# A recurrent segment kernel on one core: another order of the items of a segment, and three edits in front of the segment loop

## The chip, the cores and the metric

The kernel runs on one core of a Trainium2 chip. The metric is the device time of one launch in microseconds (us). A core has TensorE (PE, matrix products; its weight loads are listed as PEld), VectorE (DVE), ScalarE (ACT), GpSimd (POOL) and SyncE (SP, which here only issues DMA transfers). Each engine works off its own list of instructions in order, and they wait for each other by semaphores. PSUM, where TensorE leaves its products, has eight banks; ScalarE and VectorE copy ("evacuate") them to the on-chip memory SBUF.

## What is computed

```python
def _A_ref(x, mem0, Wq, Wk, Wv, Wo, seg_len):      # x (1, 2048, 640), 32 heads of 192, 8 memory rows, seg_len 32
    L = M + seg_len
    mask = (idx[:, None] < M) | (idx[:, None] >= idx[None, :])
    mem = mem0
    for s in range(n_seg):                          # 64 segments, one after the other
        h = jnp.concatenate([mem, xs], axis=1)      # 40 rows
        q, k, v = h @ Wq, h @ Wk, h @ Wv            # 640 -> 32 x 192 each
        p = _softmax(where(mask, q k^T * scale, -1e9))
        o = einsum(p v, Wo)                         # 6144 -> 640
        mem = o[:, :M, :]                           # the memory of the next segment
        outs.append(o[:, M:, :])

g = _sigmoid((x * gate_w).sum(-1, keepdims=True))
a = _A_ref(x, A_mem0, A_Wq, A_Wk, A_Wv, A_Wo, 32)
b = (_gelu(x @ w_gate) * (x @ w_up)) @ w_down       # the FFN, 640 -> 1536 -> 640
return g * a + (1 - g) * b
```

Part "a" is a recurrence: a segment needs the 8 memory rows which the segment before left. Part "b" depends on nothing but the input.

## The kernel before

**In front of the loop.** The FFN is done first, in four blocks (`blk`) of 512 rows, and left in device memory. `ffn_transposes` (line 818, DVE) makes five transposed input tiles `xT[k]`; `ffn_gu` makes for each of twelve column tiles f a gate product G (line 828), an up product U (line 831), a GELU (line 834, ACT) and their product `hT[f]` (line 836, DVE); `ffn_down` (line 850) multiplies all twelve `hT` by `w_down` for four row tiles `a`, each one PE operation with 24 matmuls. A PE operation waits, ahead of its first matmul, for everything it reads: the first G for all five `xT`, "down 0" for all twelve `hT`.

**Main rows and left rows.** A segment has 40 rows: 24 rows of x and 8 of memory (32 "main" rows), and the last 8 rows of x, which are called "left" rows. The left rows of four segments make a group g of 32 rows. Since they don't depend on the memory, their Q and K products are made ahead, as fill, one "unit" (group, octet) at a time, and kept in a scratch in device memory; a loop over `units` in front of the segments makes the first six of them (`left_mm`, line 919; `left_rows`, evacuation on ACT, transposes on DVE). The left V products are made once for four segments, in the segment with q = s % 4 = 0 (`proj`, second loop), but those of its first octet already in the segment before, as items "vb" (`vl_mm`, line 1092). Segment 0 has none before it and makes its own in its group 1, evacuated by DVE (`vl_evac`, line 1086).

**The segment loop.** 64 segments; heads go in four octets of eight, from 0 to 3 in even segments and from 3 to 0 in odd ones. A segment runs through a list of items, written out by hand or by a search: `PROG` for q = 0, 1, 2 and `PROG3` for q = 3. The code walks the list and hands each item's operations to the engines' queues, so the list is the order on every engine at once, and of the DMA issues on SP too:

- `g n k`: step k of five of the projection group n. `GROUPS` says which: group 0 is Q and K of octet 0, group 1 V of octet 0 with Q and K of octet 1, group 2 V 1 with Q 2 and K 2, group 3 V 2 and Q 3, group 4 K 3, group 5 V 3. Each of a group's products is four matmuls of 32-wide tiles side by side (line 1119, and line 226 where the weights stay). After step 4 ACT evacuates Q and K (line 1140) and V (line 1143).
- `tq i`, `tk i`: DVE transposes the Q or K rows of octet i (line 1154), POOL copies a part of Q (line 1157).
- `sc i`: scores of octet i on PE (lines 1165 to 1180), maximum and subtraction on DVE (lines 1192, 1194); POOL fills in the left Q and K of the next octet (line 976). `ex i`: exponential on ACT (line 1204), sum and normalization on DVE (line 1206 and on).
- `pt i`: transposes of the probabilities on PE (lines 1227 and 1232), evacuated by ACT (line 1245; octet 3 partly by DVE). `pv i`: probabilities times V with 64-wide tiles (lines 1260, 1262), evacuated to "U" by ACT (line 1278; octet 3 partly by DVE, line 1283).
- `wo i 0`, `wo i 1`: half of the output product of octet i; 64-wide in q = 3 (line 1339, where main and left rows go together), 32-wide else (line 1296; line 1321 for octet 3).
- `lf q u k`, `le q u m`: step k of a left unit, and its evacuation, in segments with that q only. `vb k`: as above, in q = 3.

**The seam.** After the last item, DVE and ACT collect the output product (lines 1506, 1509), DVE transposes the new memory rows into the input of the next segment (line 1517) and PE goes on with its first projections.

**The weights.** Not all of Wq, Wk, Wv and Wo fits into SBUF: 13 pieces of Q, K, V (384 KB each) and 3 of Wo (480 KB each) of octet 0 share their places with those of octet 3. As soon as a piece has been used for the last time in a segment, `swap_loads` issues on SP the load of the piece that shares its place (`load_piece`, line 628), so that every segment loads 16 pieces. An octet that ends a segment begins the next, so its pieces are there.

**PSUM banks** are dealt out in list order: `misc_bank` takes the bank which was given out longest ago among those free for that use.

Of the kernel before, what the change touches and what calls it, by code (L numbers as in the profile page):

```python
# [3 lines left out]
ACTF = mybir.ActivationFunctionType  # L4
# [234 lines left out]
def _build(nc, A_x, A_mem0, A_Wq, A_Wk, A_Wv, A_Wo, seg_len, w_gate, w_up, w_down,  # L239
           gate_w, out, opts=None):  # L240
    opts = dict(opts or {})
    Bsz, S, Dm = A_x.shape
# [274 lines left out]
    def piece_view(key, o):  # L517
        if key[0] == 3:
# [4 lines left out]
    PROG = [("g", 0, 0), ("g", 0, 1), ("g", 0, 2), ("g", 0, 3), ("g", 0, 4), ("tq", 0), ("g", 1, 0), ("g", 1, 1),  # L523
# [12 lines left out]
    PROG3 = [("g", 0, 0), ("g", 0, 1), ("g", 0, 2), ("g", 0, 3), ("g", 0, 4), ("g", 1, 0), ("tq", 0), ("tk", 0),  # L536
# [285 lines left out]
    def ffn_gu(blk):  # L822
        for f in range(FT):
            if blk + 1 == NFB and f and f % (FT // NH) == 0:
# [3 lines left out]
            S_.add("pe", [lambda e, k=k, f=f, gb=gb: e.matmul(ps[:, gb, 0:FB], wg_sb[NH * f // FT][:, k, f * 128 % FH:f * 128 % FH + 128], xT_sb[:, k, :],  # L828
                                                              start=(k == 0), stop=(k == KT - 1)) for k in range(KT)],
                   reads=[r_wg[NH * f // FT]] + r_xT, writes=[r_ps[gb]], name="ffn G %d %d" % (blk, f))  # L830
# [12 lines left out]
    def ffn_down(blk):  # L843
        n1 = min(Dm, 512)
        for a in range(FA):
            xb = 3 + 2 * (a % 2)
            yb = xb + 1
            fns = []
            for f in range(FT):
                fns.append(lambda e, f=f, a=a, xb=xb: e.matmul(ps[:, xb, 0:n1], hT_sb[:, f, a * 128:(a + 1) * 128], wd_sb[:, f, 0:n1],  # L850
                                                               start=(f == 0), stop=(f == FT - 1)))
                if Dm > 512:
                    fns.append(lambda e, f=f, a=a, yb=yb: e.matmul(ps[:, yb, 0:Dm - 512], hT_sb[:, f, a * 128:(a + 1) * 128], wd_sb[:, f, 512:Dm],
                                                                   start=(f == 0), stop=(f == FT - 1)))
            wr = [r_ps[xb]] + ([r_ps[yb]] if Dm > 512 else [])
# [89 lines left out]

    units = [(0, NOCT - 1)] + [(1, o) for o in LUNIT[3].values()] + [(0, 1), (0, 2), (0, 0)]
    for n, (g, o) in enumerate(units):
# [10 lines left out]
        left_store(g, o, b)  # L958
        if n == 0:
# [120 lines left out]
    def vl_evac(s, o, bk, eng="dve"):  # L1080
        out, in_ = vl_sb[o].rearrange("p (c n) -> p c n", c=3), ps[:, bk, 0:384].rearrange("p (n c) -> p c n", c=3)
        if eng == "act":
            S_.add("act", lambda e: e.activation(out=out, in_=in_, func=ACTF.Copy),
                   reads=[r_ps[bk]], writes=[r_vl[o]], name="Vl evac s%d o%d" % (s, o))
        else:
            S_.add("dve", lambda e: e.tensor_copy(out=out, in_=in_),  # L1086
                   reads=[r_ps[bk]], writes=[r_vl[o]], name="Vl evac s%d o%d" % (s, o))

    def vl_mm(s, k):
# [519 lines left out]
```

## Time and profile before

| | us |
|---|---|
| runs before: 1717.53, 1730.37, 1730.9; median | 1730.37 |
| the profiled execution, its time | 1724.01 |
| its span | 1722.3 |
| granted TensorE clock, mean | 0.995 |
| in front of the first segment | 177.3 |
| segments 0 to 62 | 1507.5 |
| segment 63, the last | 37.5 |

The lower three rows are windows of the profiled execution, cut at the first matmul of segments 0 and 63. Line numbers in the profile are those of the kernel before. A row of the profile's windows gives, for a stretch of time, the busy time of each engine and its number of instructions, then the granted clock (1 is full speed), the share of time in which the 16 DMA engines were busy, and what they moved. A row of the timeline gives start, duration, engine, line, operation, output and input, their shapes, how many instructions were put together, and in brackets the idle time in front and what ended it. A row of the waits gives engine, line, what it waited for, total us, how often, and the longest.

### The profile page before, as it was taken

The numbers are of one execution on the slowest core, as the hardware profiler recorded it, in microseconds if no ns is written. First come the engines' busy times: TensorE is split into PE (matmuls) and PEld (weight loads), VectorE is DVE, ScalarE is ACT, GpSimd is POOL, SyncE is SP. The second block draws the span as 40 slices with busy tenths as digits, with TensorE's granted clock in tenths as the row PEclk, the third lists the DMA queues.
The fourth block names the chain that finished last, engine by engine and source line by source line (L and its number), as shares of the span: only waits on it lengthen the run. The fifth ranks groups of instructions, "written<-read, shape, count | busy, mean of one in ns | idle before, by whom it ended". The sixth has DMA issues, their size and how long they took to land.

```text
span 1722.3 us, 75547 instructions
## 1 busy us (share of the span) xinstructions
PE 1587.5 (92%) x37107; PEld 778.1 (45%) x28147; DVE 1003.5 (58%) x2976; ACT 776.6 (45%) x1825; POOL 548.6 (32%) x1609
## 2 busy tenths in 40 slices
PE   9999899999999999999999899999999999999986
PEld 4444345444444444454444444454544444444443
DVE  5552666566565665655656656566665656555653
ACT  2222454545454454445444444445444544445442
POOL 1100233233333233333333333333333332333332
PEclk9999999999999999999999999999999999999998
DMA  9915988988888898879888898888888888988884
GB/s 298 326 37 153 342 311 296 322 308 297 297 299 319 307 323 281 305 276 329 295 287 302 294 333 281 283 288 319 310 298 288 296 316 289 310 280 303 314 313 170
DMA packets 278102, 499.27 MB, mean 290 GB/s; under 512 B 113951, under 2 KB 139015, under 8 KB 277767
## 3 DMA queue, kind: packets, MB, share of 16 engines
q1 hardware_dynamic: 249928, 482.45, 81.0%
q10 hardware_dynamic: 27839, 11.99, 2.5%
q8 instruction: 255, 4.18, 1.0%
q14 instruction: 80, 0.66, 0.1%
HBM read 473.25 MB, written 21.09 MB: 287 GB/s over the span
## 4 chain that ended last, share of the span: by engine, by line
PE 73%; DMA 12%; DVE 6%; ACT 4%; issue 3%; POOL 1%; SPq 0%; POOLq 0%; DVEq 0%; ACTq 0%
PE ps L1119 20%; PE ps L226 18%; DMA arena<-in_A_Wo_dram 6%; PE ps L1339 6%; PE ps L1296 5%; PE ps L1260 3%; PE ps L831 3%; PE ps L828 3%; PE ps L1165 3%; DMA arena<-in_A_Wv_dram 3%; PE ps L850 2%; PE ps L919 2%; PE ps L1173 1%; DMA arena<-in_A_Wk_dram 1%; ACT arena L1143 1%
## 5 line engine op out<-in xcount | busy, mean ns | idle before, releaser
L1119 PE MATMUL ps<-arena 128*32 128x384 bf16 x8660 | 650.9, 329 | 57.7 <-DVE arena L1517 47.4
L226 PE MATMUL ps<-arena 128*32 128x384 bf16 x8960 | 651.4, 326 | 7.7 <-DVE arena L1086 1.1
L1119 PEld LDWEIGHTS ps<-arena 128*32 128x32 bf16 x8660 | 221.7, 96 | 422.2 <-issue 265.6
L1154 DVE STREAM_TRANSPOSE arena<-arena 128x384 bf16<-128x384 bf16 x512 | 274.6, 561 | 125.8 <-ACT arena L1140 124.8
L1140 ACT ACTIVATE arena<-ps 128x384 bf16<-128x384 f32 x512 | 230.3, 493 | 233.8 <-PE ps L1119 223.3
L1296 PE MATMUL ps<-arena 128*32 128x320 bf16 x3456 | 187.1, 299 | 14.7 <-issue 13.4
L1157 POOL COPY arena<-arena 64x160 bf16<-64x160 bf16 x256 | 81.3, 318 | 374.3 <-DVE arena L1154 366.7
L1278 ACT ACTIVATE arena<-ps 128x480 bf16<-128x480 f32 (+1 forms) x256 | 137.6, 537 | 119.3 <-PE ps L1262 116.4
L1192 DVE TENSOR_REDUCE arena<-ps 104x4 f32<-104x160 f32 x256 | 82.9, 324 | 162.7 <-PE ps L1180 162.7
L1143 ACT ACTIVATE arena<-ps 128x384 bf16<-128x384 f32 x256 | 124.8, 488 | 106.9 <-PE ps L1119 105.3
L1245 ACT ACTIVATE arena<-ps 128x448 bf16<-128x448 f32 x192 | 104.6, 545 | 125.8 <-PE ps L1232 125.8
L1204 ACT ACTIVATE ps<-ps 104x160 f32<-104x160 f32 x256 | 75.8, 296 | 139.0 <-DVE ps L1194 137.1
L1206 DVE TENSOR_REDUCE arena<-ps 104x4 f32<-104x160 f32 x256 | 82.4, 322 | 95.7 <-ACT ps L1204 94.6
L976 POOL COPY arena<-arena 128x96 bf16<-128x96 bf16 x256 | 71.4, 279 | 201.2 <-PE ps L1180 163.8
L1296 PEld LDWEIGHTS ps<-arena 128*32 128x32 bf16 x3456 | 97.4, 96 | 68.2 <-issue 26.2
L1339 PE MATMUL ps<-arena 128*64 128x320 bf16 x1536 | 124.6, 305 | 1.2 <-ACT arena L1278 0.9
L1286 POOL COPY arena<-arena 128x96 bf16<-128x96 bf16 x192 | 51.3, 267 | 228.8 <-ACT arena L1278 222.6
L1260 PE MATMUL ps<-arena 128*64 128x160 bf16 x1536 | 118.3, 240 | 3.4 <-issue 3.3
L919 PE MATMUL ps<-arena 128*32 128x384 bf16 x1280 | 110.4, 328 | 0.0
L1262 PE MATMUL ps<-arena 128*64 128x64 bf16 x1536 | 104.2, 193 | 1.6 <-issue 1.3
L1260 PEld LDWEIGHTS ps<-arena 128*64 128x64 bf16 x1536 | 81.5, 109 | 47.5 <-ACT arena L1143 19.7
L1339 PEld LDWEIGHTS ps<-arena 128*64 128x64 bf16 x1536 | 79.9, 111 | 34.2 <-issue 10.4
(100 smaller groups left out, 2320.6 us busy)
## 6 DMA issues: line engine op xcount, KB each, us to landing
arena<-in_A_Wk_dram SPq DMA_DIRECT2D x335, 384.0 KB, 6.6
arena<-in_A_Wv_dram SPq DMA_DIRECT2D x335, 384.0 KB, 8.6
arena<-in_A_Wo_dram SPq DMA_DIRECT2D x205, 480.0 KB, 5.6
arena<-in_A_Wq_dram SPq DMA_DIRECT2D x209, 384.0 KB, 5.0
arena<-left_qk_scratch SPq DMA_DIRECT2D x126, 96.0 KB, 5.0
left_qk_scratch<-arena ACTq DMA_DIRECT2D x45, 192.0 KB, 4.1
left_qk_scratch<-arena SPq DMA_DIRECT2D x30, 96.0 KB, 4.5
ffn_b_scratch<-arena ACTq DMA_DIRECT2D x16, 160.0 KB, 3.1
```

The costliest lines, as they stand in the source:

```text
L226: return e.add_instruction(mybir.InstMatmult(name=nm, start_tensor_calc=like["start"], stop_tensor_calc=stop, tile_size=(128, 32), tile_po ...
L919: fns.append(lambda e, outp=outp, rhs=rhs, j=j: e.matmul(outp, lhs, rhs, start=(k == 0), stop=(k == KT - 1), tile_position=(0, 32 * j)))
L1119: fns.append(lambda e, outp=outp, rhs=rhs, j=j: e.matmul(outp, lhs, rhs, start=(k == 0), stop=(k == KT - 1), tile_position=(0, 32 * j)))
L1140: S_.add("act", lambda e, m=m, bk=bk: e.activation(out=rows_sb[m], in_=ps[:, bk, 0:384], func=ACTF.Copy), reads=[r_ps[bk]], writes=[r_rows ...
L1143: S_.add("act", lambda e, i=i, bk=bk: e.activation(out=v_sb[i % NVB].rearrange("p (c n) -> p c n", c=3), in_=ps[:, bk, 0:384].rearrange("p ...
L1154: S_.add("dve", lambda e: e.transpose(out=dst[:, :, 0:L], in_=rows_sb[m].rearrange("p (c r) -> p c r", r=L)), reads=[r_rows[m]], writes=[r ...
L1245: S_.add("act", lambda e: e.activation(out=PT, in_=ps[:, bank, 0:PTW + 128], func=ACTF.Copy), reads=[r_ps[bank]], writes=[r_PT], name="pT ...
L1260: return [lambda e: e.matmul(full, v[:, e0:e0 + 64], PTm[:, i], start=True, stop=False, tile_position=(0, 64 * i), skip_group_check=True), ...
L1262: lambda e: e.matmul(part, vl[:, e0:e0 + 64], PTl[:, i], start=False, stop=True, tile_position=(0, 64 * i), skip_group_check=True)]
L1278: S_.add("act", lambda e: e.activation(out=apx(u[:, 0, 0, :], [[rs, na], [3 * rs, 4], [1, R]]), in_=ps[:, A, 0:na * W].rearrange("p (c t r ...
L1296: fns.append(lambda e, i=i, t=t, j=j, gv=gv: e.matmul(ps[32 * j:32 * j + 32, bank, 0:2 * DJ].rearrange("p (h n) -> p h n", h=2), lhs2[i], ...
L1339: S_.add("pe", [lambda e, i=i, g_=g_, c=c, p=p: e.matmul(ps[64 * i:64 * i + 64, LB, 0:2 * DJ], U3[:, p % 4, c, :], g_[:, c, 2 * DJ * i:2 * ...
```

## The change

Both lists are replaced. In `PROG`, all five steps of group 1 stand together ahead of "sc 0"; "tk 0" comes before "tq 0"; "sc 1" and "pt 0" move behind the last step of group 2; "tq 3" moves ahead of "pv 1"; the two halves "wo 0 0" and "wo 0 1" come closer together, with the first between the last two steps of group 4, and the second behind the last of them; "wo 1 0" and "wo 1 1" stand together; the left steps ("lf") and evacuations ("le") are spread in another way. In `PROG3`, "pv 0" stands right behind "sc 1", "wo 0 0" soon behind "sc 2", "wo 0 1" and "pv 1" behind the last step of group 4, and the five "vb" steps all stand behind "wo 3 1".

In front of the loop: the very first gate product (block 0, f = 0) becomes five operations, each of which reads only its own `xT[k]`; in each block "down 0" becomes two operations, the first of which reads the first eleven `hT` and the second all twelve; the left V products of octet 0 of segment 0 are made in the loop over units, after the third unit, in bank 1, and evacuated by ACT, so that segment 0 needs no case of its own in `proj`.

```diff
@@ -520,28 +520,28 @@
         return bview(o, GQ)
 
     GROUPS = [[(0, 0), (1, 0)], [(2, 0), (0, 1), (1, 1)], [(2, 1), (0, 2), (1, 2)], [(2, 2), (0, 3)], [(1, 3)], [(2, 3)]]
-    PROG = [("g", 0, 0), ("g", 0, 1), ("g", 0, 2), ("g", 0, 3), ("g", 0, 4), ("tq", 0), ("g", 1, 0), ("g", 1, 1),
-            ("tk", 0), ("g", 1, 2), ("sc", 0), ("g", 1, 3), ("ex", 0), ("g", 1, 4), ("g", 2, 0), ("g", 2, 1),
-            ("g", 2, 2), ("lf", 1, 0, 0), ("pt", 0), ("tq", 1), ("tk", 1), ("sc", 1), ("g", 2, 3), ("g", 2, 4),
-            ("tq", 2), ("ex", 1), ("lf", 2, 1, 0), ("lf", 1, 0, 1), ("lf", 1, 0, 2), ("pv", 0), ("g", 3, 0),
-            ("tk", 2), ("g", 3, 1), ("g", 3, 2), ("g", 3, 3), ("pt", 1), ("lf", 2, 1, 1), ("g", 3, 4), ("sc", 2),
-            ("ex", 2), ("lf", 2, 1, 2), ("pv", 1), ("g", 4, 0), ("g", 4, 1), ("lf", 0, 1, 0), ("g", 4, 2),
-            ("lf", 1, 0, 3), ("lf", 1, 0, 4), ("lf", 1, 1, 0), ("lf", 2, 1, 3), ("lf", 1, 1, 1), ("le", 1, 0, 0),
-            ("wo", 0, 0), ("tq", 3), ("g", 4, 3), ("le", 1, 0, 1), ("g", 4, 4), ("g", 5, 0), ("g", 5, 1),
-            ("lf", 1, 1, 2), ("lf", 0, 1, 1), ("pt", 2), ("lf", 1, 1, 3), ("wo", 0, 1), ("tk", 3), ("sc", 3),
-            ("pv", 2), ("g", 5, 2), ("wo", 1, 0), ("ex", 3), ("g", 5, 3), ("wo", 1, 1), ("g", 5, 4), ("wo", 2, 0),
-            ("pt", 3), ("lf", 0, 1, 2), ("wo", 2, 1), ("pv", 3), ("lf", 1, 1, 4), ("lf", 0, 1, 3), ("lf", 0, 1, 4),
-            ("le", 0, 1, 0), ("lf", 2, 1, 4), ("le", 2, 1, 0), ("le", 0, 1, 1), ("le", 1, 1, 0), ("le", 1, 1, 1),
-            ("wo", 3, 0), ("le", 2, 1, 1), ("wo", 3, 1)]
+    PROG = [("g", 0, 0), ("g", 0, 1), ("g", 0, 2), ("g", 0, 3), ("g", 0, 4), ("g", 1, 0), ("tk", 0), ("g", 1, 1),
+            ("tq", 0), ("g", 1, 2), ("g", 1, 3), ("g", 1, 4), ("sc", 0), ("g", 2, 0), ("tq", 1), ("g", 2, 1),
+            ("g", 2, 2), ("tk", 1), ("g", 2, 3), ("lf", 2, 1, 0), ("ex", 0), ("g", 2, 4), ("sc", 1), ("pt", 0),
+            ("lf", 2, 1, 1), ("tq", 2), ("g", 3, 0), ("lf", 1, 0, 0), ("g", 3, 1), ("ex", 1), ("lf", 2, 1, 2),
+            ("pv", 0), ("tk", 2), ("lf", 1, 0, 1), ("lf", 0, 1, 0), ("g", 3, 2), ("lf", 1, 0, 2), ("pt", 1),
+            ("g", 3, 3), ("g", 3, 4), ("lf", 1, 0, 3), ("sc", 2), ("tq", 3), ("pv", 1), ("lf", 1, 0, 4),
+            ("le", 1, 0, 0), ("g", 4, 0), ("g", 4, 1), ("g", 4, 2), ("lf", 1, 1, 0), ("lf", 1, 1, 1),
+            ("lf", 0, 1, 1), ("g", 4, 3), ("wo", 0, 0), ("ex", 2), ("le", 1, 0, 1), ("g", 4, 4), ("wo", 0, 1),
+            ("lf", 1, 1, 2), ("pt", 2), ("tk", 3), ("g", 5, 0), ("g", 5, 1), ("sc", 3), ("pv", 2), ("g", 5, 2),
+            ("g", 5, 3), ("wo", 1, 0), ("wo", 1, 1), ("ex", 3), ("g", 5, 4), ("wo", 2, 0), ("pt", 3), ("wo", 2, 1),
+            ("lf", 0, 1, 2), ("pv", 3), ("lf", 0, 1, 3), ("lf", 0, 1, 4), ("lf", 2, 1, 3), ("lf", 2, 1, 4),
+            ("le", 0, 1, 0), ("le", 0, 1, 1), ("lf", 1, 1, 3), ("lf", 1, 1, 4), ("le", 2, 1, 0), ("le", 1, 1, 0),
+            ("le", 2, 1, 1), ("wo", 3, 0), ("le", 1, 1, 1), ("wo", 3, 1)]
     PROG3 = [("g", 0, 0), ("g", 0, 1), ("g", 0, 2), ("g", 0, 3), ("g", 0, 4), ("g", 1, 0), ("tq", 0), ("tk", 0),
-            ("g", 1, 1), ("g", 1, 2), ("sc", 0), ("g", 1, 3), ("ex", 0), ("g", 1, 4), ("tq", 1), ("g", 2, 0),
-            ("tk", 1), ("g", 2, 1), ("g", 2, 2), ("g", 2, 3), ("g", 2, 4), ("sc", 1), ("tk", 2), ("g", 3, 0),
-            ("pt", 0), ("tq", 2), ("g", 3, 1), ("g", 3, 2), ("g", 3, 3), ("ex", 1), ("pv", 0), ("g", 3, 4),
-            ("sc", 2), ("pt", 1), ("ex", 2), ("g", 4, 0), ("g", 4, 1), ("wo", 0, 0), ("g", 4, 2), ("g", 4, 3),
-            ("g", 4, 4), ("tq", 3), ("tk", 3), ("wo", 0, 1), ("pv", 1), ("sc", 3), ("g", 5, 0), ("pt", 2),
-            ("wo", 1, 0), ("wo", 1, 1), ("ex", 3), ("pv", 2), ("g", 5, 1), ("g", 5, 2), ("g", 5, 3), ("pt", 3),
-            ("wo", 2, 0), ("g", 5, 4), ("wo", 2, 1), ("pv", 3), ("vb", 0), ("vb", 1), ("vb", 2), ("wo", 3, 0),
-            ("wo", 3, 1), ("vb", 3), ("vb", 4)]
+            ("g", 1, 1), ("g", 1, 2), ("g", 1, 3), ("sc", 0), ("ex", 0), ("g", 1, 4), ("g", 2, 0), ("tq", 1),
+            ("tk", 1), ("g", 2, 1), ("g", 2, 2), ("g", 2, 3), ("pt", 0), ("g", 2, 4), ("sc", 1), ("pv", 0),
+            ("tq", 2), ("g", 3, 0), ("g", 3, 1), ("g", 3, 2), ("tk", 2), ("g", 3, 3), ("ex", 1), ("g", 3, 4),
+            ("sc", 2), ("tq", 3), ("wo", 0, 0), ("pt", 1), ("g", 4, 0), ("g", 4, 1), ("g", 4, 2), ("ex", 2),
+            ("g", 4, 3), ("g", 4, 4), ("wo", 0, 1), ("pv", 1), ("tk", 3), ("pt", 2), ("g", 5, 0), ("sc", 3),
+            ("wo", 1, 0), ("ex", 3), ("wo", 1, 1), ("pv", 2), ("g", 5, 1), ("g", 5, 2), ("g", 5, 3), ("pt", 3),
+            ("wo", 2, 0), ("g", 5, 4), ("wo", 2, 1), ("pv", 3), ("wo", 3, 0), ("wo", 3, 1), ("vb", 0), ("vb", 1),
+            ("vb", 2), ("vb", 3), ("vb", 4)]
     PROGS = (PROG, PROG, PROG, PROG3)
     assert NOCT == 4
@@ ffn_gu
-            S_.add("pe", [lambda e, k=k, f=f, gb=gb: e.matmul(ps[:, gb, 0:FB], wg_sb[NH * f // FT][:, k, f * 128 % FH:f * 128 % FH + 128], xT_sb[:, k, :],
-                                                              start=(k == 0), stop=(k == KT - 1)) for k in range(KT)],
-                   reads=[r_wg[NH * f // FT]] + r_xT, writes=[r_ps[gb]], name="ffn G %d %d" % (blk, f))
+            for ks in [(k,) for k in range(KT)] if blk + f == 0 else [tuple(range(KT))]:
+                S_.add("pe", [lambda e, k=k, f=f, gb=gb: e.matmul(ps[:, gb, 0:FB], wg_sb[NH * f // FT][:, k, f * 128 % FH:f * 128 % FH + 128], xT_sb[:, k, :],
+                                                                  start=(k == 0), stop=(k == KT - 1)) for k in ks],
+                       reads=[r_wg[NH * f // FT]] + [r_xT[k] for k in ks], writes=[r_ps[gb]], name="ffn G %d %d" % (blk, f))
@@ ffn_down
+            wr = [r_ps[xb]] + ([r_ps[yb]] if Dm > 512 else [])
             fns = []
             for f in range(FT):
+                if a == 0 and f == FT - 1:
+                    S_.add("pe", fns, reads=[r_wd] + r_hT[:f], writes=wr, name="ffn down %d %d" % (blk, a))
+                    fns = []
...
-            wr = [r_ps[xb]] + ([r_ps[yb]] if Dm > 512 else [])
             S_.add("pe", fns, reads=[r_wd] + r_hT, writes=wr, name="ffn down %d %d" % (blk, a))
@@ the loop over units in front of the segments (vl_mm and vl_evac, unchanged, are defined above it now)
     units = [(0, NOCT - 1)] + [(1, o) for o in LUNIT[3].values()] + [(0, 1), (0, 2), (0, 0)]
     for n, (g, o) in enumerate(units):
         b = n % 4
...
         left_store(g, o, b)
+        if n == 2:
+            lb["v"] = 1
+            for k in range(KT):
+                vl_mm(0, k)
+            vl_evac(0, octet(0, 0), lb.pop("v"), "act")
@@ proj: three places, each now without s == 0
-                if mi[0] == 2 and s % 4 == 0 and (s == 0 or mi[1]):
+                if mi[0] == 2 and s % 4 == 0 and mi[1]:
...
-            if m == 2 and s % 4 == 0 and (s == 0 or i):
+            if m == 2 and s % 4 == 0 and i:
...
-            if s % 4 == 0 and (s == 0 or i):
+            if s % 4 == 0 and i:
```

More of the change, by code (lines that the diff above doesn't have):

```diff
@@ L944, in unit_piece, with vl_evac, vl_mm @@
         return piece_view(key, res_off[key]), r_res[key]
+    def vl_evac(s, o, bk, eng="dve"):
+        out, in_ = vl_sb[o].rearrange("p (c n) -> p c n", c=3), ps[:, bk, 0:384].rearrange("p (n c) -> p c n", c=3)
+        if eng == "act":
+            S_.add("act", lambda e: e.activation(out=out, in_=in_, func=ACTF.Copy),
+                   reads=[r_ps[bk]], writes=[r_vl[o]], name="Vl evac s%d o%d" % (s, o))
+        else:
+            S_.add("dve", lambda e: e.tensor_copy(out=out, in_=in_),
+                   reads=[r_ps[bk]], writes=[r_vl[o]], name="Vl evac s%d o%d" % (s, o))
+    def vl_mm(s, k):
+        o, bk, b = octet(s, 0), lb["v"], s // 4 % 2
+        g_, rg_ = unit_piece((2, o, k))
+        S_.add("pe", [lambda e, j=j: e.matmul(
+            ps[32 * j:32 * j + 32, bk, 0:384], XLg[b][:, k, :], g_[:, 384 * j:384 * (j + 1)], start=(k == 0), stop=(k == KT - 1),
+            tile_position=(0, 32 * j)) for j in range(4)],
+            reads=[rg_, r_XLg[b]], writes=[r_ps[bk]], name="Vl s%d o%d k%d" % (s, o, k))
     units = [(0, NOCT - 1)] + [(1, o) for o in LUNIT[3].values()] + [(0, 1), (0, 2), (0, 0)]
@@ L1078, in apx @@
         return bass.AP(ap.tensor, ap.offset, [list(ap.ap[0])] + [list(d) for d in dims])
[L1080 to L1089, printed above, removed]
-        o, bk, b = octet(s, 0), lb["v"], s // 4 % 2
-        g_, rg_ = unit_piece((2, o, k))
-        S_.add("pe", [lambda e, j=j: e.matmul(
-            ps[32 * j:32 * j + 32, bk, 0:384], XLg[b][:, k, :], g_[:, 384 * j:384 * (j + 1)], start=(k == 0), stop=(k == KT - 1),
-            tile_position=(0, 32 * j)) for j in range(4)],
-            reads=[rg_, r_XLg[b]], writes=[r_ps[bk]], name="Vl s%d o%d k%d" % (s, o, k))
     def proj(s, item):
```

## The prediction, made before the changed kernel was run

> **What bounds the kernel now.** I read the page first, then one window per kind of segment, then the queue that issues the loads, then TensorE's waits. From the page:
>
> ```profile
> span 1722.3 us, 75547 instructions
> ...
> PE 1587.5 (92%) x37107; PEld 778.1 (45%) x28147; DVE 1003.5 (58%) x2976; ACT 776.6 (45%) x1825; POOL 548.6 (32%) x1609
> ...
> q8 instruction: 255, 4.18, 1.0%
> ...
> PE 73%; DMA 12%; DVE 6%; ACT 4%; issue 3%; POOL 1%; SPq 0%; POOLq 0%; DVEq 0%; ACTq 0%
> ```
>
> TensorE is busy 92% of the span and holds 73% of the chain of waits; DMA holds 12%. So 1722.3 - 1587.5 = 134.8 us are left in which TensorE has nothing, and the change does not remove matmuls: all it can win lies in these and in the small change-over times inside "busy". Four consecutive segments (q = 0, 1, 2, 3, the columns being length, then busy time of PE, PEld, DVE, ACT, POOL, then granted clock, DMA share, GB/s):
>
> ```profile
> 653.11:677.64 24.53, 22.66 (x612) 11.62 (x473) 16.81 (x50) 11.50 (x28) 8.13 (x25) 1.00 0.83 277
> 677.64:701.84 24.20, 22.19 (x592) 10.36 (x433) 14.79 (x46) 12.23 (x29) 7.34 (x24) 1.00 0.89 304
> 701.84:724.71 22.87, 21.08 (x553) 9.72 (x414) 13.76 (x44) 11.36 (x27) 8.15 (x25) 1.00 0.90 314
> 724.71:748.77 24.06, 22.96 (x508) 12.00 (x388) 12.24 (x41) 10.95 (x27) 10.04 (x27) 1.00 0.87 314
> ```
>
> No other engine is near its limit, but DMA is at 83 to 90%: each segment swaps 16 pieces. Around the moment at which the loads of Wo are issued, in six-microsecond windows of q = 0, 1, 2 and in one of two microseconds, the pipe looks like this (same columns):
>
> ```profile
> 665.11:671.11 6.00, 5.80 (x172) 3.87 (x160) 3.73 (x11) 3.49 (x9) 1.11 (x4) 1.00 0.94 334
> 689.64:691.64 2.00, 2.00 (x56) 0.89 (x38) 1.43 (x6) 1.75 (x5) 0.77 (x3) 1.00 1.04 407
> 689.64:695.64 6.00, 5.25 (x149) 2.83 (x119) 4.16 (x12) 3.16 (x8) 1.09 (x4) 1.00 0.91 306
> 713.84:719.84 6.00, 5.40 (x147) 3.13 (x135) 3.82 (x13) 2.85 (x7) 1.38 (x5) 1.00 1.04 385
> ```
>
> The pipe carries 407 GB/s when it has work, and falls to 306 in q = 1 and 334 in q = 0 while it waits for Wo slots to be given free; against 407 that is 6 x (1 - 306/407) = 1.5 us lost in q = 1, 1.1 in q = 0, 0.3 in q = 2. TensorE's waits say who pays (total us, times, longest), first as PE then as weight loads:
>
> ```profile
> PE ps L1119 <- DVE arena L1517: 47.4, 63, 1.1
> PE ps L1296 <- issue: 13.4, 18, 1.5
> PE ps L1321 <- DMA arena<-in_A_Wo_dram: 11.6, 20, 1.6
> ...
> PE ps L1119 <- ACT arena L1140: 5.4, 16, 0.9
> ```
>
> ```profile
> PEld ps L1321 <- DMA arena<-in_A_Wo_dram: 16.1, 22, 1.8
> ```
>
> The 47.4 us are the seam between segments (the new memory transposed, L1517); no edit shortens that chain. The last Wo piece costs 11.6 to 16.1 us (one wait seen from two sides), evacuations before the next projection 5.4.
>
> **Part 1, the q = 3 list.** "pv 0" moves right behind "sc 1", "wo 0 0" right behind "sc 2", and "vb 0" to "vb 2" from between "pv 3" and "wo 3 0" to the end. All three put 64-wide tiles next to each other, where 32-wide projections stood between. What a change of shape costs, in a q = 3 segment (start, duration):
>
> ```profile
> 832.26 1.01 PE L1339 MATMUL ps<-arena 128*64 128x320 bf16 x12
> 833.20 0.67 PE L1119 MATMUL ps<-arena 128*32 128x384 bf16 x12
> ...
> 842.26 1.82 PE L1339 MATMUL ps<-arena 128*64 128x320 bf16 x24
> 844.01 0.51 PE L1092 MATMUL ps<-arena 128*32 128x384 bf16 x8
> 845.14 0.35 PE L1119 MATMUL ps<-arena 128*32 128x384 bf16 x4 [0.62 <-DVE arena L1517]
> ```
>
> Twelve Wo matmuls take 833.20 - 832.26 = 0.94 us to the next shape, twenty-four 844.01 - 842.26 = 1.75; the difference, 0.81, is twelve matmuls alone, so one change costs 0.94 - 0.81 = 0.13 and there-and-back about 0.25. Two such pairs go (pv 0, wo 0 0): -0.5. The third pair (vb) I cost at nothing: today the three vb steps lie over the evacuation of the last U tile, and "wo 3 0" will wait for it bare. The five vb steps then all lie behind the last Wo matmul. From there to the next segment's first matmul is 844.01 to 845.14 = 1.13 us, spent on the transposed memory; five steps at 0.16 (next fence) are 0.8, so that wait still hides them. Sum: -0.5 x 15 segments with vb = **-7.5 us**. Bounds: 0 (if pv 0 finds its probabilities late) to 0.75 x 15 = -11.
>
> **Part 2, the list of q = 0, 1, 2.** Three things happen to it. First, Wo pieces are asked for sooner: "wo 0 1" stood behind g 5 1 and two or three left steps and now stands right behind g 4 4. A step of four projection matmuls is 0.16 (start to start of the first two rows):
>
> ```profile
> 682.43 0.34 PE L1119 MATMUL ps<-arena 128*32 128x384 bf16 x4
> 682.59 0.75 PE L226 MATMUL ps<-arena 128*32 128x384 bf16 x8
> 683.18 0.33 PE L1119 MATMUL ps<-arena 128*32 128x384 bf16 x4
> ```
>
> In q = 1 "wo 0 1" comes six to seven steps sooner, 1.07 us; in q = 0 and 2 four to five, 0.75. In q = 1 that is most of the 1.5 us which the pipe loses, and its share of the wait for the last piece is the largest. SP issues the same loads in the same order, so nothing new stands in front of them; the load of the FFN rows that hangs on "wo 0 1" moves up with it, and POOL's copies go with their "pv" and "tq" steps, on an engine that is busy 8 of 24 us. I take 11 of the 16.1 us; bounds 0 (the pipe is then simply full, as in q = 2) and -16.
>
> Second, the bank reuse at the start of g 1: in the row of 682.59 eight matmuls take 0.59 to the next row, where two steps are 0.33, so 0.26 is a wait for the evacuation of a bank; the like in q = 0 is the row of 5.4 us. With all of g 1 together and the banks taken in another order these waits mostly go: I take -5 of 5.4, and -2 of 0.26 x 32 = 8.3 in q = 1 and 2. Bounds 0 and -13.7.
>
> Third, new waits. "pt 0" now stands behind g 2 4, so on ScalarE the evacuation of the transposed probabilities is queued behind three evacuations of group 2, and "pv 0" waits for it; and "sc 3" follows its K rows more closely (by two steps in q = 0 and 1). No row shows this order. From the rows of rival C below I take +0.1 a segment, 48 segments, **+5**, because the work in between still about covers the chain; bounds 0 and +29. Sum of part 2: -11 - 5 - 2 + 5 = **-13 us**.
>
> A rule of the Trainium skill bears on the first item: "SBUF — State Buffer", section "Summary: rules for kernel authors", has one estimate an HBM-to-SBUF transfer with about 358 GB/s. By it q = 1's 304 x 24.20 = 7.36 MB would be an estimated 20.5 us of pipe against 18.1 at 407, and the pipe, not the request, would be late, as in rival B. The trace goes beyond it: 407 GB/s for two microseconds, 385 for six.
>
> **Part 3, the repairs in front of the loop.** A row of the start, two of the first segment, and the group of the down matmuls:
>
> ```profile
> 9.08 1.69 PE L828 MATMUL ps<-arena 128*128 128x512 bf16 x5 [2.07 <-DVE arena L818]
> ```
>
> ```profile
> 184.08 0.49 PE L226 MATMUL ps<-arena 128*32 128x384 bf16 x8 [1.05 <-DVE arena L1086]
> 185.43 0.51 PE L1119 MATMUL ps<-arena 128*32 128x384 bf16 x8 [0.86 <-ACT arena L1140]
> ```
>
> ```profile
> L850 PE MATMUL ps<-arena 128*128 128x512 bf16 x192 | 52.6, 379 | 3.3 <-DVE arena L836 3.3
> ```
>
> "Down a=0" waits 3.3 us in four blocks for the last column tile of h; with only its last matmuls waiting, eleven of twelve tiles run in that time: -3.3. The first gate started when all five transposes were done, 2.07 us late; it can now follow them one by one, and what it saves is about the four steps which then lie over them, less the last transpose: -0.9 (bounds 0 and -2.07). The left V of segment 0 leaves its group 1 for the units loop, which has free banks, and with it go the waits of 1.05 and 0.86; its 20 matmuls stay, at the same price, in front. I take -1.1 (bounds 0 and -1.9). It goes to ScalarE, which at that place evacuates two left products at a time; no row shows a shortage there. Sum **-5.3 us**.
>
> **Sum.** -7.5 - 13 - 5.3 = -25.8. The profiled execution took 1724.0 (span 1722.3 and 1.7 around it), so 1698.2; the median of the runs, 1730.4, is 6.4 above it: **1705 us**, -1.5%. I take the measurement to tell about 1% (17 us) from no change.
>
> **Rival B: the pipe stays the pace.** If the Wo pieces land no sooner, because the pipe is merely emptied earlier and the last request (which hangs on "wo 2 0", hardly moved) still sets the end, part 2 gives 0 and the sum is -7.5 - 5.3 = -13: 1717, within 1%. For it: q = 2 with 385 GB/s and no gap waits as well. Against it: the gap in q = 1.
>
> **Rival C, slower: the queue of ScalarE.** In q = 1, ScalarE and one wait of the scores of octet 3 for their K rows:
>
> ```profile
> 688.83 0.54 ACT L1245 ACTIVATE arena<-ps 128x448 bf16<-128x448 f32 x1 [0.95 <-PE ps L1232]
> 689.27 0.48 ACT L1143 ACTIVATE arena<-ps 128x384 bf16<-128x384 f32 x1
> 689.64 0.50 ACT L1140 ACTIVATE arena<-ps 128x384 bf16<-128x384 f32 x1
> ...
> 694.65 0.28 PE L1173 MATMUL ps<-arena 128*40 128x40 bf16 x8 [0.44 <-DVE arena L1154]
> ```
>
> The probabilities' evacuation takes 0.54; three others in front at a pitch of 0.37 to 0.50 make 1.65 to 2.04 us, and between "pt 0" and "pv 0" lie only about 1.8 us of TensorE work. The wait of 0.44 of the scores grows where K rows come two steps (0.33) nearer. If both bite, 0.6 x 48 = +29; then the requests of Wo, which follow "wo 0 0", are late too and part 2's gains fall away: 1730.4 - 13 + 29 = 1746, and 1754 if q = 3's gain fails with them. It decides when "pv 0" waits over 0.3 us in each segment. Against it: ACT is busy 12 of 24 us in these segments.
>
> **Rival D: instruction fetch.** 13.4 us of waits have no releaser at all ("issue", L1296); the queue of instructions moves 255 packets of 4.18 MB, 16 KB each, and the stalls may fall at other places in another order, under a wait or in the open: -8 to +8 us on the forecast's 1705. On that the Trainium skill, "Runtime: NRT & Kernel Launch", section "Instruction fetch mechanics", says that crossing a block boundary is mostly hidden; by this nothing would move. The trace shows up to 1.5 us in the open.
>
> **Chances.** Forecast 0.50, B 0.25, C 0.17, D 0.08. Faster by over 1% (under 1713): nearly all of the forecast, a third of D, a little of B: 0.51. Slower by over 1% (above 1748): about half of C and a part of its worse end, a trace of B and D: 0.13. Within 1%: 0.36. The forecast's own range is 1690 to 1715 (all bounds of parts 1 and 3, half of those of part 2). Held to 8 in 10 it must reach B and the nearer half of C: 1687 to 1738.
>
> **What would show it.** Right: q = 3 segments at 23.0 instead of 23.5 to 24; the waits of L1321's line for Wo under 6 us; the 3.3 us in front of the down matmuls and the rows of 5.4 and 1.05 gone. Wrong: a new PE wait for the evacuation of probabilities before "pv 0" (rival C), the DMA share at 407 GB/s throughout with Wo waits unchanged (B), or "issue" waits that grow (D). A larger span in front of segment 0 would refute part 3.

## The result and the profile after

The changed kernel takes 1731.07 us (median of 22 runs, 1726.01 to 1739.89); the kernel before, run on the same chips, 1722.58 (22 runs, 1708.92 to 1730.93). The ratio is 1.0052, 95% interval 1.0035 to 1.0069: half a per cent slower, where 1.5% faster was forecast. Two of the three runs of before that the prediction had lie at the upper end of what that kernel does, so its 1730.4 started 8 us too high.

The profiled execution of the changed kernel is the slowest of its 22 runs (1739.89), so its waits are shown for their kind and place, and their sizes are checked below on other executions. From its page:

```profile
span 1738.1 us, 75810 instructions
...
PE 1574.0 (91%) x37090; PEld 766.5 (44%) x28147; DVE 991.1 (57%) x2975; ACT 787.7 (45%) x1826; POOL 550.9 (32%) x1609
```

The span has grown by 15.8 us and TensorE's busy time has fallen by 13.5: TensorE stands still longer. Where? Segments 20 to 23, which answer to the four shown in the prediction, and segment 24, which has q = 0 again (length, then the busy times, granted clock, DMA share, GB/s; these windows are cut 0.2 us behind each segment's first matmul):

```profile
659.39:683.72 24.33, 22.26 (x620) 11.04 (x476) 16.53 (x51) 11.86 (x28) 8.20 (x25) 1.00 0.82 277
683.72:709.30 25.58, 21.82 (x600) 10.37 (x436) 14.57 (x46) 12.37 (x29) 8.00 (x24) 1.00 0.93 307
709.30:731.13 21.83, 20.36 (x560) 9.49 (x416) 13.57 (x44) 11.54 (x27) 7.82 (x24) 1.00 0.85 305
731.13:755.75 24.62, 22.34 (x516) 11.96 (x392) 12.24 (x41) 10.94 (x27) 9.76 (x27) 1.00 0.84 307
755.75:783.88 28.13, 23.64 (x620) 11.93 (x476) 16.38 (x51) 11.83 (x28) 7.94 (x24) 0.94 0.70 241
```

and segment 24 of the kernel before:

```profile
748.77:774.19 25.42, 22.38 (x612) 11.46 (x473) 16.50 (x50) 11.55 (x28) 7.47 (x24) 1.00 0.77 261
```

Two segments of the same kind and the same list, 20 and 24, take 24.33 and 28.13 us. The list is the same, so the list alone doesn't make the difference. TensorE's waits in the changed kernel (total us, times, longest):

```profile
PE ps L1128 <- DVE arena L1526: 38.1, 55, 1.1
PE ps L1330 <- DMA arena<-in_A_Wo_dram: 16.7, 23, 2.3
PE ps L1330 <- issue: 14.1, 14, 1.9
...
PE ps L1348 <- ACT arena L1287: 8.5, 15, 0.6
PE ps L923 <- issue: 8.0, 5, 2.6
PE ps L1269 <- issue: 6.2, 10, 2.2
PE ps L1128 <- issue: 5.8, 8, 1.3
PE ps L226 <- ACT arena L1287: 5.3, 14, 0.4
```

All rows with "<- issue" (no releaser) together make 46.2 us here (the expectations below quote the larger ones among them, 44, or the count from matmul start to matmul start, 60); in the kernel before they made 25.0. Of the 46.2, 32 lie in segments with q = 0 (14 of the 25.0 before). The waits for weights in flight (rows "<- DMA" of Wq, Wk, Wv, Wo) went from 15.6 to 22.1. The row of 5.4 us, evacuations in front of a projection, is gone, as forecast, and a new one of nearly the same size has come (5.3: a bank of the first left products in q = 0, still being evacuated as U).

What a wait without a releaser looks like, at the end of segment 24 (start, duration):

```profile
770.80 0.33 PE L1128 MATMUL ps<-arena 128*32 128x384 bf16 x2
772.22 0.83 PE L1128 MATMUL ps<-arena 128*32 128x384 bf16 x14 [1.09 <-issue]
...
776.38 0.34 PE L923 MATMUL ps<-arena 128*32 128x384 bf16 x4
778.98 0.33 PE L226 MATMUL ps<-arena 128*32 128x384 bf16 x4 [2.27 <-issue]
```

The first stop is in the middle of a step (two of its matmuls are done), the second in the middle of a left step, behind its matmuls for Q and ahead of those for K. Now the stretch from the end of the one to the end of the other, and the start of what follows, in windows:

```profile
772.20:778.97 6.77, 4.49 (x128) 2.98 (x128) 2.37 (x8) 2.13 (x5) 1.38 (x3) 1.00 0.68 223
```

```profile
779.85:781.15 1.30, 1.30 (x20) 0.42 (x12) 0.96 (x3) 0.49 (x2) 0.47 (x2) 0.50 0.04 13
```

128 matmuls and 128 weight loads are 256 instructions to the one. The page before had 255 packets of instructions with 4.18 MB, 16.4 KB each; the page of the changed kernel has 37090 matmuls and 28147 weight loads on record, 65237, which over 255 packets is 255.8 each. Counted through the whole trace, weight loads included, all 57 waits without a releaser stand at one and the same place modulo 256, to within one instruction; so do all 39 of the kernel before, at another place. So TensorE's program comes in blocks of 256, one packet each, and it stops where a block ends and the next one is not there. It used up this block in 4.5 us and then waited 2.3. The record of the next block's packet fits: it started at 776.71, 4.5 us after this block began, took 0.97, and TensorE went on 1.3 us after its end. The second row shows an after-effect: behind the stop the granted clock is 0.50 for a while.

### The profile page after: what moved, and what is told of

Its sections match the earlier page's. It is cut to its first block, busy times and chain, and to the rows that moved or that the text cites. A ratio compares the mean times of both kernels' runs of the same rounds, so it can differ in the third digit from the quotient of the medians.

```text
span 1738.1 us, 75810 instructions
## 1 busy us (share of the span) xinstructions
PE 1574.0 (91%) x37090; PEld 766.5 (44%) x28147; DVE 991.1 (57%) x2975; ACT 787.7 (45%) x1826; POOL 550.9 (32%) x1609
## 3 DMA queue, kind: packets, MB, share of 16 engines
q8 instruction: 255, 4.18, 0.9%
## 5 line engine op out<-in xcount | busy, mean ns | idle before, releaser
L1305 PE MATMUL ps<-arena 128*32 128x320 bf16 x3456 | 168.8, 299 | 4.1 <-issue 1.5
L1348 PE MATMUL ps<-arena 128*64 128x320 bf16 x1536 | 124.7, 304 | 10.8 <-ACT arena L1287 8.5
L1305 PEld LDWEIGHTS ps<-arena 128*32 128x32 bf16 x3456 | 95.2, 97 | 45.5 <-ACT arena L1248 12.7
L1271 PE MATMUL ps<-arena 128*64 128x64 bf16 x1536 | 108.4, 194 | 6.9 <-POOL arena L1283 4.2
L1348 PEld LDWEIGHTS ps<-arena 128*64 128x64 bf16 x1536 | 82.6, 110 | 33.7 <-ACT arena L1287 13.4
```

The lines of the kernel that those rows point to most:

```text
L1271: lambda e: e.matmul(part, vl[:, e0:e0 + 64], PTl[:, i], start=False, stop=True, tile_position=(0, 64 * i), skip_group_check=True)]
L1305: fns.append(lambda e, i=i, t=t, j=j, gv=gv: e.matmul(ps[32 * j:32 * j + 32, bank, 0:2 * DJ].rearrange("p (h n) -> p h n", h=2), lhs2[i], ...
L1348: S_.add("pe", [lambda e, i=i, g_=g_, c=c, p=p: e.matmul(ps[64 * i:64 * i + 64, LB, 0:2 * DJ], U3[:, p % 4, c, :], g_[:, c, 2 * DJ * i:2 * ...
```

## Experiments

Two theories stood against each other. Theory F: the new order does remove the waits that it was forecast to remove, but TensorE then comes to the end of a block before the next has been fetched, and the fetch is late because its packets queue behind the weights. The rivals: the order itself has worse waits (rival C), or the late Wo pieces are all of it (rival B). Every ratio below is to the kernel before on the same chip.

**One part of the change at a time.** e1: the old lists with the new code in front of the loop. e2, e3: the kernel before with one list replaced.

```diff
e1:  open change, but PROG and PROG3 as before
e2: -PROG = [before]      e3: -PROG3 = [before]
    +PROG = [after]           +PROG3 = [after]
```

> The old lists with the three repairs in front of the loop. Both theories: the first segment starts 3.7 us sooner than before (173.6 against 177.3 in the two traces), nothing else moves, so about 4 us under the kernel before. If the repairs move where TensorE's instruction blocks begin inside the segments, the waits without a releaser may shift by a few us either way.

> The kernel before with the new list for q = 0, 1, 2 alone. Theory F (instruction fetch): waits for results fall, but TensorE then reaches the end of an instruction block before the next block is there; waits without a releaser grow by about 15 us, mostly in q = 0, and the waits for Wo do not fall: 8 to 14 us slower than before. My forecast had -13 us for this part. Rival C (queue of ScalarE): slower too, but with a named wait in front of pv 0 in each segment.

> The kernel before with the new list for q = 3 alone. My forecast had -7.5 us. Theory F: the saved changes of tile shape are given back as waits without a releaser at Wb p15, V o0 k1 and pT o2 (8 us in the trace of the changed kernel): -2 to +5 us against before.

e1: 0.9978 (0.9961 to 0.9994), some 4 us faster. e2: 1.0014 (0.9992 to 1.0036). e3: 1.0026 (0.9999 to 1.0053). Neither list gains what was forecast for it, and e2 is less slow than expected. The waits without a releaser are 26.6, 34.0 and 31.8 us; those for weights 14.1, 22.1 and 18.0. Each list raises both, and TensorE hardly waits for the evacuated probabilities in front of "pv" (rows of 0.5 us, two times, in e2 and in the changed kernel; none in e3), where rival C needed over 0.3 us in each segment: it falls here.

**Less traffic, same instructions.** e5 and e6 are the two kernels with the swap loads cut.

```diff
 def load_piece(key, name):
+    cut = (lambda v: v) if name == "res" else (lambda v: v[:, 0:1] if key[0] == 3 else v[:, 0:384])
-    ... e.dma_start(piece_view(key, res_off[key]), piece_src(key)) ...
+    ... e.dma_start(cut(piece_view(key, res_off[key])), cut(piece_src(key))) ...
```

> The kernel before, but each swap load in the segments brings only a quarter of a Q, K or V piece and a third of a Wo piece (the rest of the weights of octets 0 and 3 stays what it was, so the output is not the reference's). TensorE's instructions are the same, one for one. Theory F and rival B agree that the waits for Wo (11.6 us) go; theory F adds that the waits without a releaser (25 us by the page) all but go, because the instruction packets no longer stand behind the pieces: 35 to 45 us faster than before in all. Without theory F: 12 to 15 us faster.

> The changed kernel with the same short swap loads. Theory F: with the late instruction blocks and the late Wo pieces gone, only the waits for results are left, in which the new order is the better one: 20 to 30 us faster than the kernel before with short loads, as my forecast had it for the full loads. Rival C (the new order has waits of its own): no faster than that kernel, or slower.

e5: 1667.06 us, 0.9651 (0.9613 to 0.9689); e6: 1640.23, 0.9501 (0.9470 to 0.9533). With the traffic gone the new order is 26.8 us faster than the old one. From the page of e6:

```profile
span 1639.0 us, 75810 instructions
...
PE 1535.8 (94%) x37090; PEld 759.1 (46%) x28147; DVE 988.3 (60%) x2975; ACT 787.0 (48%) x1826; POOL 548.9 (33%) x1609
```

from the page of e5:

```profile
PE 1566.9 (94%) x37090; PEld 773.0 (46%) x28147; DVE 1003.0 (60%) x2976; ACT 776.5 (47%) x1825; POOL 549.4 (33%) x1609
```

and the head of e6's list of TensorE's waits:

```profile
PE ps L1129 <- DVE arena L1527: 50.3, 53, 1.1
PE ps L1349 <- ACT arena L1288: 8.6, 15, 0.6
PE ps L226 <- ACT arena L1288: 5.8, 15, 0.4
PE ps L1190 <- POOL arena L1284: 5.7, 1, 5.7
```

No row for weights is left, and 0.6 us without a releaser (e5: none). The old order lost more to the traffic than expected (58 us, not 35 to 45). The number of instructions and of packets is the same in e6 as in the changed kernel; only the bytes beside them fell, from 482 to 177 MB on the weights' queue. The packets' records in the trace say how. For the blocks that begin between 5 and 19 us after their segment does, the next block's packet starts 3.0 us after the block begins in the changed kernel (mean of 150) and 0.45 in e6 (of 153); it takes 1.03 and 1.08 us; and in the changed kernel no block of segments 0 to 62 was entered less than 1.18 us after its packet's end. There 105 of 243 blocks were entered within 1.7 us of their packet's end, that is, about as soon as they could be. In e6 two were.

Where the 26.8 us lie is not where the forecast looked for them. In e5 TensorE stands still for 1667.9 - 1566.9 = 101.0 us, in e6 for 1639.0 - 1535.8 = 103.2. The rows of waits that went (the bank reuse in front of a projection, half of the scores' wait for K, the waits in front of the loop) were replaced by new ones (for U, for POOL, for a bank in q = 0), and all of the gain stands inside TensorE's busy time, 31.1 us less for the same matmuls: changes of shape, and waits too short or too well covered to have a row. (A busy time on the page counts a matmul up to its modelled end, so a short wait behind it is hidden.)

This also gives the pace: the four segments 20 to 23 of before hold 3973 TensorE instructions, 15.5 blocks in 95.66 us, 6.2 us a block, while a fetch takes 3.0 + 1.0 + 1.2 = 5.2 us on the average in mid-segment and up to 6.8 in the stop above, from block to block. The fetch lies just under the pace of the work; an order that packs a block's work tighter runs into it.

On this the Trainium skill, "Runtime: NRT & Kernel Launch", section "Instruction fetch mechanics", has the 256 instructions in 16 KiB, and says that the crossing is mostly hidden; beside loads at this rate it is not.

**Only the loads of Wo cut** (e12: as e6, but `name == "res" or key[0] < 3` is loaded whole).

> The changed kernel, with the swap loads of Wo alone cut to a third (the rest of those weights stays what it was, so the output is not the reference's); those of Q, K and V are whole. The waits for Wo (17 us by the page) go. Theory F: the waits without a releaser stay where the Q, K and V pieces are in flight and fall where only Wo was: of 44 us 15 to 30 stay, and the kernel is 30 to 45 us faster than the changed one, well short of the 91 of all loads cut. If the late Wo pieces were the whole cause: 17 us faster and no more, with the waits without a releaser as they were.

1677.71 us, 0.9710 (0.9686 to 0.9735): 53 us under the changed kernel by the medians and 59 by the ratios, more than the 30 to 45 expected and far more than the 17 which the late Wo pieces alone would give. Waits for weights fell to 7.1 and those without a releaser to 16.4. The place of these stops tells which ones went: those that begin 17 us or more after their segment's start, when the pieces of Wo are in flight, make 32 us in the changed kernel and 1 in e12, those before 14 and 15. So the loads of Wo hold up the packets at the end of a segment, beside being late themselves.

**Where the blocks begin.** n one-column matmuls behind the warm-up compute nothing that is used and push every later instruction 2n places on:

```diff
     warm(14)
+    S_.add("pe", [lambda e: e.matmul(ps[0:1, 4, 0:1], ident[:, 0:1], ident[:, 0:1], start=True, stop=True) for _ in range(n)],
+           reads=[r_ident], writes=[r_ps[4]], name="pad")
```

> The changed kernel with 72 one-column matmuls (144 TensorE instructions, weight loads counted) added behind the warm-up, which compute nothing that is used. Theory F: all block boundaries move by 144 of 256 instructions inside the segments; the waits without a releaser leave the places where they stand now (Vl o3 k0, LK o3 k2, PV o3, Wb p15) and stand 144 instructions earlier; their sum changes by 8 to 28 us, up by my estimate from the trace. Rival (order of the list, the DMA pipe): these waits stay at their places and the time is that of the changed kernel plus the pad's own 1 to 5 us in front.

> As the kernel with 72 extra matmuls, with 24 (48 instructions, 0.19 of a block). Theory F: the waits without a releaser stand 48 instructions earlier in the segments than in the changed kernel; their sum lies between those of the changed kernel (44 us by the page) and of the one with 72 (39 us) or up to 10 us beside them; time 1720 to 1740. Rival (no part played by the blocks): the waits stay where they are and the time is that of the changed kernel, 1731.

> The same with 48 (96 instructions, 0.38 of a block): the waits without a releaser stand 96 instructions earlier than in the changed kernel; time 1720 to 1740.

> The same with 104 (208 instructions, 0.81 of a block): the waits without a releaser stand 208 instructions earlier, or 48 later; time 1720 to 1745. Taken with the other pads it tells how much of the changed kernel's loss hangs on where the blocks begin, and how much on the order as such.

> The changed kernel once more. If its place in the blocks is an unlucky one: again 0.3 to 0.7% slower than before, about 0.8% above its padded forms. If the difference between it and its padded forms was one of chips: 0.2 to 0.3% faster than before, as they were.

> The kernel before with 48 extra one-column matmuls behind the warm-up. If the old order stood at a lucky place: 3 to 10 us slower than before, with more waits without a releaser than its 25 us. If the old order doesn't care: within 3 us of it.

> The kernel before with 104 of them: the same two cases at another place of the blocks.

| kernel | ratio to before | interval | no releaser, us | for weights, us |
|---|---|---|---|---|
| before | 1 | | 25.0 | 15.6 |
| before, 48 (e14) | 1.0063 | 1.0034 to 1.0091 | 33.2 | 16.1 |
| before, 104 (e15) | 1.0018 | 0.9996 to 1.0039 | 29.8 | 12.7 |
| changed | 1.0052 | 1.0035 to 1.0069 | 46.2 | 22.1 |
| changed again (e13) | 1.0035 | 1.0011 to 1.0059 | 48.9 | 25.8 |
| changed, 24 (e9) | 0.9973 | 0.9958 to 0.9989 | 37.4 | 22.1 |
| changed, 48 (e10) | 0.9972 | 0.9947 to 0.9996 | 30.9 | 25.3 |
| changed, 72 (e4) | 0.9986 | 0.9961 to 1.0012 | 38.8 | 21.8 |
| changed, 104 (e11) | 0.9980 | 0.9953 to 1.0007 | 33.3 | 22.9 |

(The last two columns add up the rows of one profiled execution each.) The stops moved with the padding. Segment 24 of e4:

```profile
783.74 0.35 PE L1130 MATMUL ps<-arena 128*32 128x384 bf16 x4 [1.20 <-issue]
...
787.40 0.48 PE L226 MATMUL ps<-arena 128*32 128x384 bf16 x4
787.57 0.80 PE L1332 MATMUL ps<-arena 128*32 128x160 bf16 x30
788.86 0.52 PE L1332 MATMUL ps<-arena 128*32 128x160 bf16 x18 [0.49 <-issue]
```

```profile
783.60:788.85 5.25, 4.63 (x134) 3.05 (x122) 2.68 (x9) 2.78 (x6) 2.26 (x5) 1.00 0.55 200
```

The left steps run through, the stops stand elsewhere (the second in the middle of the last Wo products), and between them lie 134 + 122 = 256 instructions once more. So an edit that adds work and changes nothing in the segments is worth up to 0.8% (1.0052 to 0.9972): the changed kernel stood at the worst of its five places, the kernel before at the best of its three. My estimate for e4 had the wrong sign (up, measured down from 46.2 to 38.8); that the sum hangs on the place was right, which places are good was not foreseen. At the same padding the new order is the better one: 0.9972 against 1.0063 with 48, 0.9980 against 1.0018 with 104. (The same padding isn't the same place, since the code in front differs too.) Over the places tried the new kernel averages 0.9991 and the old 1.0027, some 6 us by this estimate, of which e1 gives 4 to the code in front: with full loads the lists gain next to nothing on the average of these places, and the place decides the sign. What is left without a releaser at a good place, in e10:

```profile
PE ps L1332 <- issue: 7.4, 7, 1.7
...
PE ps L925 <- issue: 6.0, 6, 1.8
...
PE ps L226 <- issue: 3.5, 3, 1.7
```

e9 and e10 are faster than both kernels, by 0.3% against before.

**Smaller transfers**, in the hope that a packet then waits less: each swap load in two, by columns (e7) or by partitions (e8).

```diff
+cuts = first and second 768 columns of Q, K, V (c = 0, 1 and c = 2 of Wo)      # e7
+cuts = partitions 0 to 63 and 64 to 127                                        # e8
+for each cut: S_.add("sp", ... e.dma_start(cut of the view, cut of the source) ...)
```

> The changed kernel with each swap load split into two transfers, by columns (1536 bytes a row instead of 3072; the same bytes in all). If an instruction packet waits behind a fixed number of pieces' rows or transfers, its wait (3 to 4 us in the middle of a segment) halves, the waits without a releaser (60 us over the segments by my count) fall to 10 to 20, and the kernel is 20 to 35 us faster than the changed one, if the pipe keeps its rate. SP issues twice as many transfers. If the packet waits for bytes in flight whatever their cut, or the stalls have another cause: no change, or slower by SP's issues.

> The changed kernel with each swap load split into two transfers by partitions (64 rows of 3072 bytes each). If the packet waits behind a number of transfers, the same gain as with the split by columns; if behind a number of rows or bytes, no gain in the stalls; the pipe and SP are loaded as in the other split.

1928.23 us (1.1178, 1.1119 to 1.1237) and 2320.57 (1.3443, 1.3384 to 1.3501). The packets did wait less, about 2 us instead of 3, far fewer blocks were entered at once (22 of 243 in e7 and under ten in e8 instead of 105), and the waits without a releaser fell to 1.9 and 0.0 us. This agrees with the Trainium skill, "DMA: Bandwidth & Descriptors", section "Queues, rings and completion order", by which a DMA engine turns to another queue only when it is through with a packet of descriptors of the first. It isn't shown by these runs alone, for the pipe carried less beside the packets too. And it got slower than that was worth: TensorE's waits for weights rose from 22.1 to 186.3 and 429.8 us. 100 us in the middle of e7, and of e8, after it:

```profile
700.00:800.00 100.00, 86.01 (x2168) 41.22 (x1644) 54.61 (x170) 45.85 (x108) 31.14 (x92) 0.97 0.83 267
```

```profile
700.00:800.00 100.00, 78.00 (x1753) 34.23 (x1313) 43.64 (x136) 36.23 (x85) 24.55 (x74) 0.86 0.88 213
```

In e8 the rows are as long as before (3072 bytes) and DMA is 88% busy at 213 GB/s, so the size of the rows isn't the reason; whether the number of transfers in flight or their 64 partitions are, these runs don't tell.

## Why the prediction was wrong

The range held the time; the sign was wrong. By its own steps:

**The step that failed** is the term for the instruction fetch, which the sum has at nothing: the prediction put it aside as a rival with "-8 to +8" (rival D, chance 0.08) and took each removed wait as time. Measured, the waits without a releaser grew by 21 us (25.0 to 46.2), and the -11 for the pieces of Wo, the largest single term, came out as +5 (11.6 to 16.7; all weights +6.5). Rival D's own sign, "issue" waits that grow, is what the trace shows; its size was too small by more than half.

The order as such is faster. In e5 and e6, where neither fetch nor weights are late, the segment starts in the traces give, summed by q = 0, 1, 2, 3 and for the time in front (q = 3 with the last segment): old 374.9, 373.3, 353.8, 389.0 and 176.9; new 375.8, 366.0, 341.9, 381.5 and 173.8. The new order loses 0.9 in q = 0 and gains 7.3 in q = 1, 11.9 in q = 2, 7.5 in q = 3, 3.1 in front: 28.9 us. That this comes near the forecast's 25.8 is luck: 11 of these were waits for Wo, which the short loads take from both kernels, and the rest was to come in good part from rows of waits, whose sum didn't fall (101.0 to 103.2). With full loads the same sums are 397.2, 388.7, 365.0, 394.1, 177.3 and 414.0, 388.9, 362.4, 399.3, 173.4: 16 us lost. (By the same starts segment 63 of the kernel before begins at 1682.7, not at the 1684.8 of the table of the time before.) Of the difference of some 45 the rows without a releaser (+21) and those for weights (+6.5) show 28. The granted clock could make most of what is left in these two executions: a mean of 0.986 of 1738 us is 24 us of clock lost, 0.995 of 1722 is 9 (an estimate from the means).

**Part 1 (q = 3): half of its size.** Of the 7.5 us, the fifteen segments with vb, to which the forecast gave -7.5, bring 4.1 (352.3 to 348.2 with short loads, 0.27 each), and the last segment, which the forecast didn't count, the other 3.4. The bare wait for U that was costed at nothing is the row L1348 of 8.5 us (15 times 0.57). It is paid for as said: the wait in the seam of these segments falls from 9.7 to 1.0 us with short loads. What the sum didn't have is a wait for POOL inside "pv 3" (the row L1271 <- POOL arena L1283, 4.2 us, 13 times; 5.1 in e6, 0.3 before). With full loads the stops ate the gain: q = 3 is 0.4 us longer, not 0.5 shorter (median of its segments 23.9 after, 23.5 before).

**Part 2 (q = 0, 1, 2): one term wrong, one too small.** The 11 us from asking for Wo sooner did not come: the waits for Wo went from 11.6 to 16.7. The pieces were asked for sooner (by 1.4 us for the last in q = 2, 0.8 in q = 1, by the medians of the issue times), and landed at 21.1 us after the segment's start instead of 21.5 in q = 2, at 22.7 instead of 22.9 in q = 1: rival B was right about that. The DMA shares in the windows that answer to those of before show how little the gaps closed (q = 0, 1, 2; 334, 306 and 385 GB/s before):

```profile
671.39:677.39 6.00, 5.83 (x176) 3.86 (x168) 3.77 (x12) 3.44 (x8) 1.34 (x5) 1.00 0.91 331
695.72:701.72 6.00, 5.32 (x147) 3.05 (x131) 4.10 (x12) 3.23 (x8) 1.07 (x4) 1.00 0.97 319
721.30:727.30 6.00, 5.66 (x157) 3.44 (x149) 3.80 (x14) 3.31 (x8) 1.47 (x5) 1.00 1.03 375
```

The other items gave more than their -7 + 5: 18 us in e6 against e5, where the weights play no part. Counted from matmul start to matmul start in q = 1 and 2, 15 us of it lie between the matmuls of the scores, of which the row of their wait for K shows 5 (9.2 to 4.1), and 13 between those of the projections; other places got dearer. So the +5 for the probabilities and the K rows was not needed, and had the wrong sign for the K rows: their wait fell with full loads too (6.6 to 3.1). The bank reuse of 5.4 us in q = 0 only changed its place: the new wait of 5.3, a bank in q = 0, was not on the list, and q = 0 gained nothing.

**Part 3 (in front): half right.** The first segment starts 3.9 us sooner in the profile after (173.4) than in the one before, and the runs of e1 give 4 us, though in the profile of e1 it starts at 176.0: without padding, the old code in front took 175.5 to 177.3 us (before, e2, e3, e5), the new 173.4 to 176.0 (changed twice, e1, e6, e12), with the 20 matmuls of the left V in it. The first gate now starts at 7.47 instead of 9.08 us. The wait in front of the down matmuls is gone, and 1.5 us have come back in a later one. The left V, forecast at -1.1, gained nothing: segment 0 has a new wait,

```profile
181.23 0.51 PE L1128 MATMUL ps<-arena 128*32 128x384 bf16 x8 [2.63 <-ACT arena L1149]
```

and on ScalarE the reason, a V evacuation that waits for the store of left products out of the buffer it is to fill, ahead of the rows' evacuation:

```profile
179.92 0.49 ACT L1152 ACTIVATE arena<-ps 128x384 bf16<-128x384 f32 x1 [3.98 <-DMA left_qk_scratch<-arena]
```

Before, other waits of 1.05 and 0.86 us stood in front of it.

**What stays open.** How much of the half per cent belongs to the stretches at half clock. The mean granted clock is 0.986 in the profiled execution of the changed kernel (0.995 before) and 0.993 in that of e13, which is as slow by the median, and 0.983 in that of e11, which took 13 us less (1726.88), so it is not the main part; it may make up some of the scatter between runs. Why some places of the blocks are good is not settled either: it would need a model of the fetch that gets e4 right.

## What to carry to other kernels

In a long unrolled program like this one, count TensorE's instructions against the fetch: where a block of 256 takes little longer than its packet needs beside the loads, a removed wait is given back at the next block's end, and the sign of a small edit is decided by where the blocks begin. Before judging an order by half a per cent, run it at several paddings; and test what it is worth as such with the traffic taken away.

## What the runs showed of the hardware

Beside the weights' loads an instruction packet started 3.0 us after its block began, on the average in mid-segment, and 0.45 with the loads cut (changed kernel, e6); no block of segments 0 to 62 was entered less than 1.18 us after its packet's end. Behind a stop of 2.27 us the granted clock was 0.50. Cutting a 384 KB load into two transfers of the same bytes, which was meant to help, took the kernel from 1731 to 1928 us (by columns) and 2321 us (by partitions).
